# Query and weight steps that wait once a tile's estimate of VectorE time is used up

## The chip, the cores and the metric

The program runs on one core of a Trainium2 chip. Its time is the device time of one execution in microseconds (us). The kernel before takes 1639.06 us, the median of three runs from 1638.23 to 1640.07.

Names of the engines: PE is TensorE, DVE is VectorE, ACT is ScalarE, POOL is GpSimd, SP is the engine that issues the DMAs. Each works through its own queue in the order in which the program wrote it, and waits for the others by semaphores.

## What is computed

Attention through 32 packed queries per head, then two feed-forward layers over 4608 tokens of width 512. Everything is float32.

```python
def sm_attn(qq, kk, vv):
    s = scale * np.matmul(qq, kk.transpose(0, 1, 3, 2))
    a = np.exp(s - np.max(s, axis=-1, keepdims=True))
    a = a / (np.sum(a, axis=-1, keepdims=True) + 1e-09)
    return np.matmul(a, vv)
p_packed = sm_attn(p, k, v)
x = sm_attn(q, p_packed, p_packed)       # 8 batches x 8 heads x 576 x 64
# x is laid out as 4608 rows of 512
xn = x / np.sqrt(np.mean(x * x, axis=-1, keepdims=True) + 1e-06) * rms_g
g, val = xn @ w_gate, xn @ w_val          # 512 -> 1536
y = (g / (1 + np.exp(-g)) * val) @ w_out  # 1536 -> 512
h = y @ w_in                              # 512 -> 2048
out = (np.maximum(h, 0) + alpha * np.minimum(h, 0)) @ w_out2
```

## The kernel before

Every product is made of three matmuls: an operand is split into a high part (ACT, line 109) and the rest (DVE, line 112, or POOL, line 361), and `mm3` multiplies high by high, high by low and low by high (lines 121 to 123).

The first feed-forward layer goes over the tokens in twelve chunks, c = 0 to 11, of 512 or 320 tokens. Chunks 0, 4, 7 and 10 have 512, the others 320. A chunk is a loop over f = 0 to 11, one tile of 128 of the 1536 hidden columns each. A tile has this backbone, in the order in which it is written:

- PE makes `ps_g` (six matmuls for 320 tokens of one batch), ACT takes its tanh (line 1057), DVE does the gate step on it (line 1062), PE makes `ps_v` (six more), DVE multiplies (line 1066), ACT and DVE split the product into `hh` and `hl`;
- PE multiplies the *previous* tile's `hh` and `hl` into the four sums `ps_y` (`blk_out(f - 1)`), 12 matmuls;
- `both` prepares the next block of output weights, `in_h` on ACT, `in_l` on POOL or, from chunk 7 on, by a load.

The rest of the work of chunks 1 to 11 is optional in each tile: it has to be done some time in the chunk, and is fitted in between.

- A *query chain* (`q_steps`) prepares 256 tokens (or 64) of the next chunk: two transposes of scores (line 623), the maximum (625), the subtraction (627), the exponential on ACT (631), the sum and its reciprocal (633 to 635), the product (637), the transpose back `A2T` (642), then matmuls with it on PE (653) and squares on ACT (677). Steps are marked by kind: E is elementwise on DVE, X is the exponential, R reads a result of PE out of PSUM, M is a maximum of the other kind of chain. The *key chain* (`k_steps`) does the same for the keys of a later batch.
- `work(f, at)` moves these chains on at four places of a tile. at = 1 lies between the tanh and the gate step, at = 2 after `hl`, at = 3 after the first `burst`, at = 4 after the second. `burst(f, 2)` and `burst(f, 3)` issue the chains' matmuls on PE, the first just before `blk_out`, the second behind it.
- `late_step` moves the conversion of the second layer's weights on by one step (`conv_late`, 113 steps in all): of every seven, three narrow 64-bit words to floats (lines 224, 228, 230, 233) and four form sums of weight blocks on POOL (line 281) and split them into `w7o` (ACT 109, DVE 112), which SP stores to DRAM (line 278). There are two buffers `w7o`: the third split waits until the first one's store has landed. A table `EVERY` says after how many tiles a step is due at the end of a tile (every tile in chunks 1, 8, 9), `TWICE` adds steps in the middle of a tile in chunks 4, 7 and 10.

The four PSUM banks that `ps_g`, `ps_v`, `ps_at` and `ps_wg` share go round in turn, so PE can't begin a block before the one four places back has been read.

The second layer (from about 916 us on) isn't touched by any of this.

Of the kernel before, what the change touches and what calls it, by code (L numbers as in the profile page):

```python
# [18 lines left out]
def attention_moe_moe2_kernel(ctx, tc, q, k, v, p, w_gate, w_val, w_out, rms_g, w_in2, w_out2, alpha, out):  # L19
    nc = tc.nc  # L20
    B, H, S, D = q.shape
# [4 lines left out]
    T = 512  # L26
# [34 lines left out]
    tiles, of_chunk = [], []  # L61
    for t0, n, cuts in CH:
        groups = []
        for lo, hi, b in cuts:
            for o in range(lo, hi, 256):
                ids = []
# [7 lines left out]
    for i in range(NP1):  # L74
        b, r = i // 3 * 2, i % 3
# [49 lines left out]
    with tc.manual_schedule():  # L125
# [44 lines left out]
        def load_q(i):  # L170
            if i >= len(tiles):
                return
            if hold[0] is not None:
                hold[0].append(i)
                return
            t = ap.tile([128, H * D], F32, tag="q", name="qt", bufs=NQ)
            b, s = divmod(tiles[i][0], S)
            n = tiles[i][1]
            nc.sync.dma_start(
                out=t[0:n].rearrange("p (h d) -> p h d", h=H),  # L180
                in_=q[b, :, s:s + n, :].rearrange("h p d -> p h d"),
            )
            q_t[i] = t
# [157 lines left out]
        def conv(n):  # L341
            for _ in range(n):
                next(convs, None)

        def conv_to(n):
            while n_conv[0] < min(n, NU1):
                next(convs)
# [22 lines left out]
        E, X, R, M = -1, -2, -3, -4  # L370

        class Chain:
            def __init__(self, steps, b):
                self.steps, self.b, self.done, self.last = steps, b, 0, None
                self.next()

            def next(self):
                if self.kind_ok() and self.kind > 0:
                    self.done += 1
                self.kind = next(self.steps, None)  # L380
# [11 lines left out]
        chains = {"k": [], "q": []}  # L392
# [9 lines left out]
        def preload(func):  # L402
            nc.scalar.activation(out=tick[0], in_=mhalf, func=func)
# [421 lines left out]
        def hsplit(h, n):  # L825
            hh = ring.tile([128, T], F32R, tag="hh", name="hh")[:, 0:n]
            hl = ring.tile([128, T], F32R, tag="hl", name="hl")[:, 0:n]
            split_hi(hh, h)
            split_lo(hl, h, hh)
            return hh, hl  # L830
# [4 lines left out]
        def load_rows(pr, kk):  # L835
            t0, w = PAIRS[pr]
            rows = []
            for d in (kk, kk + 2):
                t = one.tile([128, 2 * T], F32, tag="w64", name="y_raw", bufs=NST)[:, 0:2 * w]
                nc.sync.dma_start(out=t, in_=y_dram[d, :, t0:t0 + 2 * w])  # L840
                rows += [t[:, 0:w], t[:, w:2 * w]]
            return rows
# [4 lines left out]
        def prep(pr):  # L847
            w = PAIRS[pr][1]

            def operand(n, kk, src):  # L850
                h, l = [p2.tile([128, T], F32R, tag=f"y{x}{n}{kk}", name="y" + x)[:, 0:w] for x in "hl"]
                split_hi(h, src)
                split_lo(l, src, h)
                y_op[OPERANDS.index(n), kk] = (h, l)

            def less(x, y):
                t = (temp() if pr == 0 else one.tile([128, T], F32, tag="w32", name="y_d", bufs=2))[:, 0:w]
                nc.vector.tensor_tensor(out=t, in0=x, in1=y, op=ALU.subtract)
                return t

            for kk in range(2):
                rows = y_rows.pop(0)
                b11, b12, b21, b22 = rows
                t1 = less(b12, b11)
                operand("b11", kk, b11)
                yield
                t2 = less(b22, t1)
                operand("t1", kk, t1)
                yield
                t4 = less(b21, t2)  # L870
                operand("t2", kk, t2)
                yield
                t3 = less(b22, b12)
                operand("t4", kk, t4)
                yield
                operand("t3", kk, t3)
                yield
                operand("b21", kk, b21)
                yield
                operand("b22", kk, b22)  # L880
                if kk == 0:
                    y_rows.append(load_rows(pr, 1))
                    yield
                yield
# [27 lines left out]
        def load_next():  # L912
            if stream:
                kind, i, n = stream.pop()
                t = wa.tile([128, 2, 256], F32R, tag="w", name="w7")
                nc.sync.dma_start(out=t.bitcast(F32), in_=(w7_dram if kind == "i" else o7_dram)[i * 7 + n])
                here.append(((kind, i, n), t))
# [10 lines left out]
        EVERY = {1: 1, 2: 2, 3: 3, 4: 1, 5: 2, 6: 3, 7: 1, 8: 1, 9: 1, 10: 1, 11: 2}  # L928
        TWICE = {4: 4, 7: 2, 10: 2}

        def late_step(c, f, mid):
            every = (TWICE if mid else EVERY).get(c)
            if every and f % every == every - 1:
                next(late, None)

        for c, (t0, n, cuts) in enumerate(CH):
            last = c == NP1 - 1
# [1 line left out]
            if c == 0:  # L939
                chains["k"] = [Chain(k_steps(b, bk_at), b) for b in range(1, B)]  # L940
            nq = [] if last else of_chunk[c + 1]
            chains["q"] = [Chain(q_steps(ids, bk_at), tiles[ids[0]][0] // S) for ids, _ in nq]

            first = [None]

            def work(f, at):
                live = [ch for ch in chains["k"] if ch.kind is not None][:1] + chains["q"]
                swap = c > 0 or at == 3 and any(ch.kind == X or ch.kind == M for ch in live)
                if swap and c == 0:
                    preload(ACTF.Exp)  # L950
                for ch in live:
                    n_ = 0
                    while n_ < 2:
                        if ch.kind == R and (at == 1 or at > 2 and (ch is first[0] or n_ == 0)):
                            pass
                        elif n_ == 0 and ch.kind == E and (c == 0 or at < 4) or swap and ch.kind in (X, M):
                            pass
                        else:
                            break
                        ch.last = (c, f, at)  # L960
                        ch.next()
                        n_ += 1
                if swap and c == 0:
                    preload(ACTF.Silu)
                if c == 0:
                    conv(2 if at < 4 else 0)
# [67 lines left out]
            for f in range(NF):  # L1034
                if c == 0 and f == 1:
                    held, hold[0] = hold[0], None
                    for i in held:
                        load_q(i)
                if c == 3 and f == 0:
                    nc.sync.dma_start(out=alpha_sb, in_=alpha.rearrange("(f p) -> p f", p=128))  # L1040
                if c == 0:
                    j1 = (f + 1) // 2
                    conv_to(min(6 * j1 + (5 if f % 2 else 6), NU1))
                if last:
                    if f == 0:
                        y_rows.append(load_rows(0, 0))
                        prepare = prep(0)
                    if f > 0:
                        next(prepare, None)
                    if f in (2, 3, 8, 9, 10):  # L1050
                        next(prepare, None)
                    if f > 2:
                        load_next()
                tg = blk_in(f, 0, "g")
                s = ring.tile([128, T], F32, tag="s", name="s")[:, 0:n]
                if c:
                    nc.scalar.activation(out=s, in_=tg, func=ACTF.Tanh, scale=0.5)  # L1057
                else:
                    nc.scalar.activation(out=s, in_=tg, func=ACTF.Silu)
                work(f, 1)  # L1060
                if c:
                    nc.vector.scalar_tensor_tensor(  # L1062
                        out=s, in0=s, scalar=1.0, in1=tg, op0=ALU.add, op1=ALU.mult
                    )
                tv = blk_in(f, 256, "v")
                nc.vector.tensor_tensor(out=s, in0=s, in1=tv, op=ALU.mult)  # L1066
                for jb in JOBS[c].get(f, ()) if c else ():
                    wg_job(*jb)
                hs[f] = hsplit(s, n)
                work(f, 2)  # L1070
                burst(f, 2)
                work(f, 3)
                late_step(c, f, True)
                if 0 < f < NF - 1:
                    blk_out(f - 1)
                if f < NF - 1:
                    burst(f, 3)
                    work(f, 4)
                if f < NF - 1:
                    both(("o", f + 1))  # L1080
                late_step(c, f, False)
            tail = [NF - 2, NF - 1]
            if nq:
                for ch in chains["q"]:
# [308 lines left out]
```

## Time and profile before

| | |
|---|---|
| median of 3 runs | 1639.06 us |
| profiled execution, its own time | 1638.71 us |
| its span, first to last instruction | 1636.9 us |
| PE busy | 1569.6 us, 96% |
| DVE busy | 1188.2 us, 73% |
| ACT busy | 891.3 us, 54% |
| POOL busy | 257.6 us, 16% |
| mean granted TensorE clock | 0.989 |

The times of the steps come from the profiled execution. PE is the engine with the least idle time; where it stands still, the views by waits and the timeline say for whom. A matmul's row in the timeline gives its start and its length; the next one's start is often earlier than its end, since matmuls overlap.

### The profile page before, as it was taken

What the parts mean: (1) busy time and instruction counts of PE and PEld (TensorE: products, weight loads), DVE (VectorE), ACT (ScalarE), POOL (GpSimd) and SP (SyncE); (2) the same over time, 40 slices, a digit from 0 to 9 for tenths busy, and PEclk for the clock granted to TensorE, in tenths of its full rate; (3) what the DMA queues carried; (4) which work ended last, traced back from release to release, by engine and by line L of the source; (5) the groups of instructions that cost most, each with busy time, mean ns of one, the idle gap of its engine ahead of it and who ended that gap; (6) DMA issues with size and microseconds to landing.
All of it is one profiled execution on the core that took longest, in us unless ns stands there. A gap on an engine that the chain in (4) does not pass through costs nothing.

```text
span 1636.9 us, 31939 instructions
## 1 busy us (share of the span) xinstructions
PE 1569.6 (96%) x11786; PEld 1377.2 (84%) x11786; DVE 1188.2 (73%) x2244; ACT 891.3 (54%) x1906; POOL 257.6 (16%) x238
## 2 busy tenths in 40 slices
PE   6689999999999999998999999999999999999999
PEld 4466887888778887888888888988998899999999
DVE  5787667666776766766766778867886787788785
ACT  4566555555465454665555546545654555565564
POOL 1442333232333312212121000000000000000000
PEclk9899999999999999999999999999999999999999
DMA  9876766626565365885645667766777667788876
GB/s 250 270 230 195 219 180 183 165 65 185 178 181 184 112 212 188 263 265 165 218 160 201 213 192 212 230 214 192 212 228 216 208 188 238 259 267 278 265 244 199
DMA packets 230426, 340.55 MB, mean 208 GB/s; under 512 B 62464, under 2 KB 96256, under 8 KB 230272
## 3 DMA queue, kind: packets, MB, share of 16 engines
q1 hardware_dynamic: 230272, 338.51, 67.0%
q8 instruction: 94, 1.54, 0.4%
q14 instruction: 60, 0.49, 0.1%
HBM read 280.77 MB, written 57.67 MB: 207 GB/s over the span
## 4 chain that ended last, share of the span: by engine, by line
PE 60%; DVE 12%; ACT 6%; issue 2%; DMA 2%; DVEq 0%; ACTq 0%; SPq 0%
PE ps_g L121 11%; PE ps_g L122 11%; PE ps_g L123 11%; PE ps_y L121 7%; PE ps_y L123 6%; PE ps_y L122 6%; DVE hl L112 2%; PE ps_wg L730 2%; PE ps_v L121 1%; PE ps_v L122 1%; PE ps_v L123 1%; DVE s L1066 1%; ACT hh L109 1%; DVE s L1062 1%; DMA w_dram<-w7o 1%
## 5 line engine op out<-in xcount | busy, mean ns | idle before, releaser
L121 PE MATMUL ps_y<-hh,in_h 128*128 128x320 f32 (+1 forms) x576 | 208.7, 362 | 4.0 <-ACT hh L109 4.0
L121 PE MATMUL ps_g<-yh,w 128*128 128x512 f32 (+1 forms) x560 | 206.5, 369 | 0.5 <-DVE tmp L1137 0.5
L122 PE MATMUL ps_g<-yl,w 128*128 128x512 f32 (+1 forms) x560 | 206.3, 368 | 0.0
L123 PE MATMUL ps_g<-yh,w 128*128 128x512 f32 (+1 forms) x560 | 205.7, 367 | 0.0
L122 PE MATMUL ps_y<-hl,in_h 128*128 128x320 f32 (+1 forms) x576 | 198.1, 344 | 3.2 <-DVE hl L112 2.6
L123 PE MATMUL ps_y<-hh,in_l 128*128 128x320 f32 (+1 forms) x576 | 196.5, 341 | 0.0
L109 ACT ACTIVATE hh<-s 128x320 fp32r<-128x320 f32 (+1 forms) x144 | 75.6, 525 | 189.5 <-DVE s L1066 189.4
L109 ACT ACTIVATE hh<-kept 128x512 fp32r<-128x512 f32 (+1 forms) x200 | 116.4, 587 | 102.1 <-PE ps_g L122 49.2
L123 PE MATMUL ps_y<-w,hl 128*128 128x256 f32 x576 | 164.7, 286 | 3.1 <-DVE hl L112 2.3
L122 PE MATMUL ps_y<-w,hh 128*128 128x256 f32 x576 | 162.7, 282 | 0.0
L121 PE MATMUL ps_y<-w,hh 128*128 128x256 f32 x576 | 162.4, 282 | 0.0
L121 PEld LDWEIGHTS ps_y<-hh,in_h 128*128 128x128 f32 x576 | 110.4, 192 | 57.8 <-issue 41.6
L361 POOL TENSOR_TENSOR in_l<-w_raw,in_h 128x512 fp32r<-128x512 f32 x72 | 95.8, 1330 | 278.7 <-ACT in_h L109 243.0
L112 DVE TENSOR_TENSOR hl<-kept,hh 128x512 fp32r<-128x512 f32 (+1 forms) x200 | 123.2, 631 | 16.0 <-ACT hh L109 14.9
L1137 DVE TENSOR_TENSOR tmp<-tmp,ps_g 128x512 f32<-128x512 f32 (+2 forms) x140 | 88.3, 631 | 55.2 <-PE ps_g L123 55.2
L112 DVE TENSOR_TENSOR hl<-s,hh 128x320 fp32r<-128x320 f32 (+1 forms) x144 | 82.5, 573 | 60.7 <-ACT hh L109 60.7
L121 PE MATMUL ps_g<-xh,wgh 128*128 128x256 f32 (+3 forms) x352 | 113.1, 321 | 10.4 <-ACT pT L116 3.2
L123 PE MATMUL ps_g<-w,hl 128*128 128x256 f32 x432 | 122.4, 283 | 0.0
L122 PE MATMUL ps_g<-w,hh 128*128 128x256 f32 x432 | 122.2, 283 | 0.0
L121 PE MATMUL ps_g<-w,hh 128*128 128x256 f32 x432 | 122.2, 283 | 0.0
L122 PEld LDWEIGHTS ps_y<-hl,in_h 128*128 128x128 f32 x576 | 110.6, 192 | 13.6 <-DVE hl L112 7.0
L1062 DVE SCALAR_TENSOR_TENSOR s<-s,ps_g 128x320 f32<-128x320 f32 (+1 forms) x132 | 70.9, 537 | 67.1 <-ACT s L1057 66.4
(197 smaller groups left out, 4204.0 us busy)
## 6 DMA issues: line engine op xcount, KB each, us to landing
w<-w_dram SPq DMA_DIRECT2D x280, 256.0 KB, 3.1
w<-o_dram SPq DMA_DIRECT2D x280, 256.0 KB, 3.0
gv_raw<-gv_dram SPq DMA_DIRECT2D x168, 256.0 KB, 3.9
in_l<-lo_dram SPq DMA_DIRECT2D x59, 256.0 KB, 3.9
w<-in_moe_w_out_dram SPq DMA_DIRECT2D x28, 512.0 KB, 5.0
w_dram<-w7o SPq DMA_DIRECT2D x56, 256.0 KB, 2.9
o_dram<-w7o SPq DMA_DIRECT2D x56, 256.0 KB, 2.6
vt<-in_v_dram SPq DMA_DIRECT2D x16, 576.0 KB, 5.9
```

The costliest lines, as they stand in the source:

```text
L109: nc.scalar.activation(out=hi, in_=src, func=ACTF.Copy)
L112: nc.vector.tensor_tensor(out=lo, in0=src, in1=hi.bitcast(F32), op=ALU.subtract)
L121: nc.tensor.matmul(out=o, lhsT=lh, rhs=rh, start=first, stop=False, skip_group_check=more)
L122: nc.tensor.matmul(out=o, lhsT=lh, rhs=rl, start=False, stop=False, skip_group_check=more)
L123: nc.tensor.matmul(out=o, lhsT=ll, rhs=rh, start=False, stop=last, skip_group_check=more)
L361: nc.gpsimd.tensor_tensor(out=l, in0=raw[u], in1=h.bitcast(F32), op=ALU.subtract)
L730: nc.tensor.matmul(out=ts[g][h * NP:(h + 1) * NP, :], lhsT=ppG[b][e * D:(e + 1) * D, c_, :], rhs=us[c_][e * D:(e + 1) * D, :], start=True, ...
L1062: nc.vector.scalar_tensor_tensor(out=s, in0=s, scalar=1.0, in1=tg, op0=ALU.add, op1=ALU.mult)
L1066: nc.vector.tensor_tensor(out=s, in0=s, in1=tv, op=ALU.mult)
L1137: nc.vector.tensor_tensor(out=out, in0=x, in1=y, op=ALU.add)
```

## The change

Three things are added. First, `spent` counts an estimate of the optional DVE time of a tile: 0.7 for each E or R step of a chain of 256 tokens (in proportion for a smaller one, 0.35 for a key chain), 0.9 for an M step, 1.0 for a late step. It is set to zero right behind the steps at at = 1. Second, an E step is only done while `spent` is under a limit: 2.2 in a chunk of 320 tokens, 3.4 in one of 512, without limit in chunks 0 and 11. R and M steps are counted and never held, X steps are neither counted nor held. Third, a late step that is due while the limit is reached is owed, and made up at the next place, which may now be the middle of a tile in any chunk.

```diff
         class Chain:
-            def __init__(self, steps, b):
-                self.steps, self.b, self.done, self.last = steps, b, 0, None
+            def __init__(self, steps, b, w=0.5):
+                self.steps, self.b, self.done, self.last, self.w = steps, b, 0, None, w
                 self.next()
...
-        def late_step(c, f, mid):
+        spent, owed = [0.0], [0]
+
+        def late_step(c, f, mid, limit):
             every = (TWICE if mid else EVERY).get(c)
-            if every and f % every == every - 1:
+            owed[0] += bool(every and f % every == every - 1)
+            if owed[0] and spent[0] < limit:
+                owed[0] -= 1
+                spent[0] += 1.0
                 next(late, None)
...
-            chains["q"] = [Chain(q_steps(ids, bk_at), tiles[ids[0]][0] // S) for ids, _ in nq]
+            chains["q"] = [
+                Chain(q_steps(ids, bk_at), tiles[ids[0]][0] // S, sum(tiles[i][1] for i in ids) / 256) for ids, _ in nq
+            ]
 
             first = [None]
+            limit = 1e9 if c == 0 or last else 2.2 if n < T else 3.4
...
-                        elif n_ == 0 and ch.kind == E and (c == 0 or at < 4) or swap and ch.kind in (X, M):
+                        elif n_ == 0 and ch.kind == E and (c == 0 or at < 4) and spent[0] < limit:
+                            pass
+                        elif swap and ch.kind in (X, M):
                             pass
                         else:
                             break
                         ch.last = (c, f, at)
+                        if ch.kind != X:
+                            spent[0] += 0.9 if ch.kind == M else 0.7 * ch.w
                         ch.next()
...
                 work(f, 1)
+                spent[0] = 0.0
...
-                late_step(c, f, True)
+                late_step(c, f, True, limit)
...
-                late_step(c, f, False)
+                late_step(c, f, False, limit)
```

What this moves is seen in the written order of two queues in chunk 9, whose 320 tokens stand beside two query chains of 256.

DVE in chunk 9, from the `hl` of tile 2 to the `hl` of tile 3, in the kernel before. `A_9376` is the first query chain, `A_9448` the second, `w_9410` and `w_9474` are late steps, lines 1062 and 1066 are the gate step and the product.

```order
L112 TENSOR_TENSOR hl<-s,hh 128x320
L627 TENSOR_TENSOR A_9376<-A_9376,s_9287 128x512
L633 TENSOR_REDUCE s_9287<-A_9376 128x16
L634 TENSOR_SCALAR s_9287<-s_9287 128x16
L635 RECIPROCAL s_9287<-s_9287 128x16
L623 STREAM_TRANSPOSE A_9448<-ps_at 128x256 x2
L230 SCALAR_TENSOR_TENSOR w_9410<-w_9021,w_9410 128x512
L224 TENSOR_SCALAR w_9474<-w_9069 128x512
L637 TENSOR_TENSOR A_9376<-A_9376,s_9287 128x512
L625 TENSOR_REDUCE s_9288<-A_9448 128x16
L1062 SCALAR_TENSOR_TENSOR s<-s,ps_g 128x320
```

The same stretch of DVE now (the second chain is called `A_9443`; the gate step is line 1075):

```order
L112 TENSOR_TENSOR hl<-s,hh 128x320
L625 TENSOR_REDUCE s_9287<-A_9376 128x16
L627 TENSOR_TENSOR A_9376<-A_9376,s_9287 128x512
L623 STREAM_TRANSPOSE A_9443<-ps_at 128x256 x2
L1075 SCALAR_TENSOR_TENSOR s<-s,ps_g 128x320
```

Nine rows stood between `hl` and the gate step; three are left. The sum, the reciprocal and the product of the first chain come a tile later, and with them its transpose back, which now follows the `hl` of tile 4 and not of tile 3. The two late steps are owed.

ACT in chunk 9, tiles 6 and 7 of the kernel before: the seven splits of one pair of weight blocks are spread over tiles 4 to 7 (two, one, two, two), and the last four stand here.

```order
L1057 ACTIVATE s<-ps_g 128x320
L109 ACTIVATE hh<-s 128x320
L109 ACTIVATE in_h<-w_raw 128x512
L109 ACTIVATE w7o<-w_9410 128x256 x2
L1057 ACTIVATE s<-ps_g 128x320
L109 ACTIVATE hh<-s 128x320
L109 ACTIVATE in_h<-w_raw 128x512
L109 ACTIVATE w7o<-w_9474 128x256 x2
```

ACT in chunk 9 now, tiles 8 and 9 and the tanh of tile 10 (line 1069 is the tanh):

```order
L1069 ACTIVATE s<-ps_g 128x320
L109 ACTIVATE hh<-s 128x320
L109 ACTIVATE w7o<-w_9538 128x256
L109 ACTIVATE w7o<-w_9598 128x256
L109 ACTIVATE in_h<-w_raw 128x512
L109 ACTIVATE w7o<-w_9598 128x256
L1069 ACTIVATE s<-ps_g 128x320
L109 ACTIVATE hh<-s 128x320
L109 ACTIVATE w7o<-w_9538 128x256 x2
L109 ACTIVATE in_h<-w_raw 128x512
L109 ACTIVATE w7o<-w_9598 128x256 x2
L1069 ACTIVATE s<-ps_g 128x320
```

The seven splits now stand in two tiles, three in tile 8 and four in tile 9, in front of the next tile's tanh.

## Rows read from the trace of the kernel before

**Rows 1.** The page: busy time, share and instructions of each engine.
```profile
PE 1569.6 (96%) x11786; PEld 1377.2 (84%) x11786; DVE 1188.2 (73%) x2244; ACT 891.3 (54%) x1906; POOL 257.6 (16%) x238
```
**Rows 2.** By stretch: PE, PEld, DVE, ACT, POOL busy, clock; chunk 9, second layer.
```profile
729.20:785.60 56.40, 51.33 (x390) 47.22 (x389) 38.22 (x85) 31.64 (x81) 10.32 (x10) 1.00 0.59 186
...
916.20:1636.90 720.70, 713.44 (x4714) 669.88 (x4712) 558.41 (x942) 389.38 (x730) 0.00 (x0) 1.00 0.73 227
```
**Rows 3.** PE's waits in chunks 1 to 10: total, times, longest.
```profile
PE ps_at L653 <- DVE A2T L642: 6.6, 3, 3.3
...
PE ps_g L121 <- DVE s L1062: 1.2, 2, 0.9
...
PE ps_at L653 <- DVE E1T L118: 0.6, 1, 0.6
```
**Rows 4.** Timeline of PE (start, length, [idle <- releaser]): chunks 3, 6, 9.
```profile
327.12 0.48 PE L653 MATMUL ps_at<-ppbd,A2T 64*128 64x128 f32 x2 [0.85 <-DVE A2T L642]
328.16 1.25 PE L653 MATMUL ps_at<-ppbd,A2T 64*128 64x128 f32 x14 [0.55 <-DVE E1T L118]
...
543.38 1.44 PE L653 MATMUL ps_at<-ppbd,A2T 64*128 64x128 f32 x16 [2.43 <-DVE A2T L642]
...
742.64 0.31 PE L121 MATMUL ps_v<-xh,wgh 128*128 128x320 f32 x1
...
746.90 0.31 PE L123 MATMUL ps_v<-xh,wgl 128*128 128x320 f32 x1
750.48 1.16 PE L653 MATMUL ps_at<-ppbd,A2T 64*128 64x128 f32 x16 [3.27 <-DVE A2T L642]
```
**Rows 5.** Timeline of ACT and DVE: chunk 9's tile 3.
```profile
743.70 0.42 ACT L1057 ACTIVATE s<-ps_g 128x320 f32<-128x320 f32 x1
...
744.49 0.65 DVE L230 SCALAR_TENSOR_TENSOR w<-w,w 128x512 int32<-128x512 int32 x1
...
745.39 1.80 DVE L637 TENSOR_TENSOR A<-A,s 128x512 f32<-128x512 f32 x1
747.12 0.67 DVE L625 TENSOR_REDUCE s<-A 128x16 f32<-128x512 f32 x1
747.71 0.47 DVE L1062 SCALAR_TENSOR_TENSOR s<-s,ps_g 128x320 f32<-128x320 f32 x1
...
749.72 0.70 DVE L642 STREAM_TRANSPOSE A2T<-A 128x512 f32<-128x512 f32 x1
```
**Rows 6.** By stretch, behind the waits of chunks 3, 6 and 9.
```profile
329.10:332.50 3.40, 3.40 (x14) 3.18 (x13) 2.94 (x5) 0.31 (x2) 1.07 (x1) 0.50 0.01 2
...
544.10:547.50 3.40, 3.40 (x19) 3.18 (x17) 2.80 (x5) 1.31 (x3) 1.28 (x1) 0.50 0.06 22
...
748.90:752.30 3.40, 1.82 (x21) 1.70 (x22) 2.29 (x4) 1.65 (x4) 0.00 (x0) 1.00 0.00 0
```
**Rows 7.** Timeline of ACT: two tanhs, and splits that wait.
```profile
773.69 0.42 ACT L1057 ACTIVATE s<-ps_g 128x320 f32<-128x320 f32 x1
...
776.71 0.42 ACT L1057 ACTIVATE s<-ps_g 128x320 f32<-128x320 f32 x1
...
765.94 0.71 ACT L109 ACTIVATE w7o<-w 128x256 fp32r<-128x256 f32 x2
...
770.32 0.42 ACT L109 ACTIVATE w7o<-w 128x256 fp32r<-128x256 f32 x1 [0.35 <-DMA o_dram<-w7o]
...
823.86 0.42 ACT L109 ACTIVATE w7o<-w 128x256 fp32r<-128x256 f32 x1
...
829.05 0.42 ACT L109 ACTIVATE w7o<-w 128x256 fp32r<-128x256 f32 x1 [3.89 <-DMA o_dram<-w7o]
```
**Rows 8.** The stores of `w7o`: from issue to landing.
```profile
DMA to landing us min/median/max: 2.0/2.7/5.8
```
**Rows 9.** Timeline of POOL in chunk 9: two adds.
```profile
745.27 1.37 POOL L233 TENSOR_TENSOR w<-w,w 128x512 int32<-128x512 int32 x1 [17.26 <-issue]
...
760.82 0.98 POOL L281 TENSOR_TENSOR w<-w,w 128x256 f32<-128x256 f32 x1
```

## The prediction

> **What bounds the kernel now.** I read the page first: PE is busy 96% of the span, DVE 73% [rows 1]. So time is won only where PE stands still. The view by stretches says where the change can act: the second layer is 720.7 us in which nothing moves, and PE is busy 713.4 of them; chunk 9 lasts 56.4 us with PE busy for 51.3, DVE for 38.2 [rows 2]. DVE has room as a mean there, so what PE loses it loses to a queue that is full for a moment. The view of PE's waits over chunks 1 to 10 names it: the largest is `A2T`, the transpose back of a query chain, three times, 6.6 us; next to it come waits for the gate step (1.2) and for a copy of a key chain (0.6) [rows 3]. The timeline puts the three waits for `A2T` into chunks 3, 6 and 9 (0.85, 2.43 and 3.27 us), each before the first matmul of line 653, and the wait for the copy behind the first of them (0.55) [rows 4]. These are the chunks of 320 tokens beside two query chains of 256.
>
> Then the timeline of DVE before the last of them shows why `A2T` was late. The tanh of tile 3 ended at 744.12, the gate step began at 747.71: 3.6 us in which DVE did a late step (744.49 to 745.39, 0.90), and then the two steps at at = 1: the product of the first chain (1.80) and the maximum of the second (0.59 until the gate step) [rows 5]. `A2T` begins 2.01 us behind the gate step's start and takes 0.70 [rows 5].
>
> **The terms.** Without these 0.90 and 2.32 (745.39 to 747.71) the gate step of tile 3 would begin at 744.49, 0.4 us behind its tanh. By the written order the change does take both away from there.
>
> How much of the wait goes? PE comes to line 653 after 30 matmuls: rest of the tile's `ps_v`, `blk_out` and the next pair, 742.64 to 746.90 plus one more of (746.90 - 742.64) / 29 = 0.147, so 4.4 us behind the end of `ps_g` [rows 4]. On DVE the way from there is tanh 0.42, then 2.01 and 0.70 [rows 5]: 3.1, with small gaps 3.2. So 1.2 us are to spare if the gate step is on time. It won't be quite: `A2T` of chunk 9 now follows tile 4, and between the gate steps of tiles 3 and 4 stand the sum, the maximum, the product and the subtraction. At start-to-start times of 1.1 for the sum with its reciprocal and 0.6 for each other (the maximum's 0.59, rows 5), 2.9, plus the 2.01, that is 4.9 us against a tile of 24 matmuls, 3.5 us: 1.4 late, 0.2 more than there is to spare. I leave 0.8 of the wait standing for gaps, and count the 0.9 that PE then waited for the gate step [rows 3] as gone: 3.27 + 0.9 - 0.8 = 3.4 us in chunk 9. In chunk 6 the transpose back stands behind two steps of 0.6 that it didn't have before it, which just uses the 1.2 up: of 2.43 I count 2.0. In chunk 3 one such step is new, and a late step and a maximum leave: of 0.85 + 0.55 I count 1.2. Sum 6.6; bounds from nothing (the wait only moves with the step) to all, 8.0.
>
> The clock. Right behind the waits of chunks 3 and 6 the granted clock was 0.50, that is 1.2 of 2.4 GHz, for 3.4 us each, with PE busy throughout; behind the longer wait of chunk 9 it stayed at 1.00 [rows 6]. At half clock such a stretch loses 1.7 us of matmuls. If the waits shrink, both can go: 3.4; since the longest wait had no fall, the tie isn't firm, and I count three quarters, 2.5. Bounds 0 and 3.4.
>
> What it adds. Late steps that are owed are made up close together. In chunk 9 the four steps that split weight blocks stood in four tiles; now seven splits stand in tiles 8 and 9, three and four, each in front of a tanh. There are two buffers, so a split waits for the store of the one two before. In the trace this took 4.1 us from start to start in chunk 9 (the second of the pair at 766.23, to 770.32) and 5.2 in chunk 10 (823.86 to 829.05), where ACT stood for 3.89 us [rows 7]; the least that the parts allow is 0.42 for the split, as much on DVE, and a landing of 2.0 [rows 8], 2.8. In chunk 10 the tile was long and hid it; here it isn't. Undisturbed, a tile of ACT and DVE takes 3.02 us from tanh to tanh with one late step in it [rows 7], PE's takes 3.5. With a pair of splits as long as a late step (0.71, rows 7), tile 8 comes to 3.4, tile 9 to 3.7, and tile 10, which gets two narrowing steps, to 3.7: 10.8 against PE's 10.6. On top come the waits: the third split would follow the first by 1.3 (its pair and one more operation of 0.6), the fifth the third by 2.6, the sixth the fourth by 1.3, the seventh the sixth at once. At 2.8 they wait 1.5 + 0.2 + 1.5 = 3.2, at 5.2 3.9 + 2.6 + 3.9 = 10.4, at 4.1 7.1. PE notices when `hl` is late by more than its reserve, which is 4.4 + 0.15 - 2.6 = 1.9 at best (the same count as above, to the end of `hl`). So PE loses 10.8 - 10.6 - 1.9 = -1.7 plus the waits: 1.5 to 8.7, 5.4 by the value of chunk 9. That value is of the second split of a pair, whose store is issued behind the first's; the first comes back sooner, so I take 4.0.
>
> The same crowding in chunk 1 (five splits in tiles 7 and 8) has tiles of 6 us and I price it at 0, at most 2. In chunks 4, 7 and 10 DVE's steps move within tiles of 7 to 9 us where no wait for `A2T` was: nothing, cover the length of the tile. In chunks 2, 5 and 8 steps move from in front of the gate step to behind `hl`; no wait of theirs is large in rows 3: nothing, bounds 1 either way. SP's stores move with their splits, and a load of `in_l` for the next block can come behind a pair of them in the middle of a tile; it is used more than half a tile later, so nothing unless the store itself waits, which is in the term above.
>
> The sum, made on the profiled execution's own 1638.71, which is 0.35 below the median: -6.6 - 2.5 + 4.0 = -5.1, so 1633.6; with the offset 1634.
>
> A rule of the Trainium skill speaks against the change here. The row: DVE's product took 1.80 us, from 745.39, beside an add on POOL from 745.27 to 746.64 [rows 5, 9], where the maximum behind it took 0.67. "SBUF — State Buffer", section "SBUF: two separate sides", says that a DVE operation with two SBUF inputs and a GpSimd operation that reads SBUF exclude each other for the whole instruction. The row agrees. By that rule the four sums of blocks that POOL does within those two tiles of chunk 9 (up to 0.98 each, rows 9) could hold up DVE by as much each time, 3.9 us in all; the sum would then be about -1.
>
> **The rivals.**
>
> *The gain is eaten.* The crowded splits cost what the waits for `A2T` give back, or PE's wait moves with `A2T`: the transpose back still comes right behind some `hl` and just before its matmuls. For it: DVE has the same number of instructions; 4.9 us against 3.5 in the one tile that matters. Against it: three of the four long stretches before a gate step get shorter by 2 us or more. Time: -9.1 + 7 to 9, or -3 + 2: 1637 to 1639, say 1638.
>
> *Slower: ACT stands behind the stores.* One mechanism, in chunk 9's tiles 8 to 10: a split that waits for a landing holds the tanh behind it, so the gate step, `hl`, and PE. At 5.2 us per buffer PE loses 8.7, and 2 in chunk 1. For it: ACT stood 3.89 us in just this pattern [rows 7]. Against it: in chunk 9 itself the wait was 0.35. It decides once it costs more than the gain: with waits for `A2T` that shrink to half (-4.0) and no clock regained, 10.7 - 4.0 = +6.7 at worst, 1645; likely 1643.
>
> *The change doesn't do what it says.* The estimate counts steps that cost DVE nothing (an R step that only ACT reads counts 0.7), so it holds steps too early, and the limits may merely shift work. Then the same as before, 1639, and the written order speaks against it, since nine rows before a gate step became three.
>
> **How the numbers follow.** What a measurement of this kernel can tell from no change is about 0.2%, 3.3 us. My forecast, 1634, has a chance of 0.54 and spreads from 1628 (all waits and both clock stretches back, 11.4, crowding at its least, 1.5) to 1636. The gain eaten: 0.22, 1638. Not doing what it says: 0.04. Slower by the stores: 0.20, 1643. Hence faster 0.53, within 0.2% 0.27, slower 0.20. The range for 8 in 10 goes from 1628 to 1643.
>
> **What would show it.** Right: in PE's waits of chunks 1 to 10 the row for `A2T` falls from 6.6 to under 2, no stretch at clock 0.50 in chunks 3 and 6, chunk 6 shorter by 3 to 4 us, chunk 3 by 2 to 3. The term of the stores: new idle time of ACT before `w7o` in chunk 9's tiles 8 and 9, 3 to 7 us, and PE waiting for `hh`, `hl` or a bank in its tiles 9 to 11. Wrong: the wait for `A2T` as long as before in tile 5 in place of 4; ACT's waits there without any of PE, which makes it faster than I say; or chunk 9 longer than 56.4 us, which makes the slower rival right.

## The result, and the profile after

The changed kernel takes 1653.28 us (median of four runs, 1652.57 to 1658.87) against 1639.23 (1638.23 to 1640.07) of the kernel before, a ratio of 1.0091 with an interval of 1.0073 to 1.0109. It is 14 us slower. 1634 was predicted, with a range from 1628 to 1643: the sign was wrong, and the time lies outside the range.

The profiled execution of the change took 1653.99 us, 15.3 more than that of the kernel before, as the spans say too (1652.2 less 1636.9). Busy time of each engine first, to be laid beside [rows 1]:

```profile
PE 1580.7 (96%) x11786; PEld 1382.5 (84%) x11786; DVE 1188.6 (72%) x2244; ACT 892.0 (54%) x1906; POOL 257.2 (16%) x238
```

The instructions are the same in number, and DVE and ACT have the same work to within 0.7 us. So nothing was added; time was lost in waiting, or at the lower clock.

A chunk runs from its first matmul to that of the next. In us, from one profiled execution of each kernel; the last two columns are two experiments of the next section:

| chunk | before | change | e3 | e11 |
|---|---|---|---|---|
| 1 | 73.98 | 73.02 | 73.12 | 72.33 |
| 2 | 66.88 | 64.35 | 65.62 | 68.56 |
| 3 | 65.98 | 62.94 | 61.22 | 61.78 |
| 4 | 88.65 | 89.54 | 88.98 | 88.80 |
| 5 | 62.93 | 65.61 | 66.60 | 66.13 |
| 6 | 62.99 | 64.75 | 61.55 | 60.76 |
| 7 | 86.08 | 88.53 | 85.38 | 85.38 |
| 8 | 57.14 | 59.98 | 58.52 | 58.04 |
| 9 | 56.42 | 60.59 | 57.22 | 52.34 |
| 10 | 79.36 | 84.38 | 80.23 | 79.54 |
| sum | 700.4 | 713.7 | 698.4 | 693.7 |

Chunks 1 to 10 lost 13.3 us. The other 2.0 lie ahead of chunk 1, in work that the change leaves in its order; they differ between executions of the experiments as well (chunk 0 began anywhere from 48.7 to 50.9 us), so I don't count them as an effect of the change. In chunks 1 to 7 the key chains' matmuls moved between chunks, so their single differences are mixed. Chunks 8 to 10 have no key chain: 12.0 us of pure loss.

The stretches of the change, in the order of columns of [rows 2]: chunks 1 to 10, chunk 9, second layer.

```profile
166.60:880.30 713.70, 684.16 (x5810) 575.58 (x5808) 478.06 (x1010) 379.15 (x913) 195.96 (x182) 0.99 0.57 180
...
735.30:795.90 60.60, 54.45 (x390) 49.60 (x389) 38.12 (x84) 33.03 (x82) 10.10 (x10) 0.95 0.55 178
...
931.40:1652.20 720.80, 713.51 (x4714) 669.86 (x4712) 558.51 (x943) 389.48 (x730) 0.00 (x0) 1.00 0.72 227
```

The second layer is unchanged to 0.1 us. Chunk 9, from which the prediction drew most of its gain, is 4.2 longer, with the same DVE time (38.1 for 38.2) and a clock of 0.95 for 1.00.

PE's waits in chunks 1 to 10 of the change, as [rows 3]:

```profile
PE ps_at L653 <- DVE A2T L642: 5.7, 3, 2.9
...
PE ps_y L122 <- DVE hl L112: 3.2, 7, 0.9
PE ps_y L121 <- ACT hh L109: 3.1, 3, 1.3
PE ps_at L663 <- DVE A2T L642: 2.1, 1, 2.1
PE ps_wg L730 <- DVE s L1075: 1.6, 1, 1.6
```

The wait for `A2T` was to fall from 6.6 to under 2. It is 5.7, and a fourth wait for a transpose back (line 663) makes it 7.8. The timeline of PE shows where the two long ones lie, in chunks 6 and 9, one tile later than in [rows 4]; that of chunk 3 is gone:

```profile
548.97 1.16 PE L653 MATMUL ps_at<-ppbd,A2T 64*128 64x128 f32 x16 [2.86 <-DVE A2T L642]
...
752.13 0.31 PE L123 MATMUL ps_g<-xh,wgl 128*128 128x320 f32 x1
...
759.36 1.91 PE L653 MATMUL ps_at<-ppbd,A2T 64*128 64x128 f32 x16 [2.51 <-DVE A2T L642]
```

Why `A2T` is late again is read from ACT and not from DVE. ACT in chunk 9, tiles 3 and 4 (line 631 is the exponential of a query chain, 1069 the tanh):

```profile
748.58 0.63 ACT L631 ACTIVATE A<-A 128x512 f32<-128x512 f32 x1 [1.88 <-DVE A L627]
749.12 0.62 ACT L109 ACTIVATE in_h<-w_raw 128x512 fp32r<-128x512 f32 x1
749.64 0.42 ACT L1069 ACTIVATE s<-ps_g 128x320 f32<-128x320 f32 x1
...
755.06 0.63 ACT L631 ACTIVATE A<-A 128x512 f32<-128x512 f32 x1 [3.39 <-DVE A L627]
755.60 0.62 ACT L109 ACTIVATE in_h<-w_raw 128x512 fp32r<-128x512 f32 x1
756.12 0.42 ACT L1069 ACTIVATE s<-ps_g 128x320 f32<-128x320 f32 x1
```

and DVE in the same tiles (line 1075 is the gate step):

```profile
750.09 0.49 DVE L1075 SCALAR_TENSOR_TENSOR s<-s,ps_g 128x320 f32<-128x320 f32 x1 [0.85 <-ACT s L1069]
...
751.71 0.49 DVE L112 TENSOR_TENSOR hl<-s,hh 128x320 fp32r<-128x320 f32 x1 [0.54 <-ACT hh L109]
752.12 0.68 DVE L633 TENSOR_REDUCE s<-A 128x16 f32<-128x512 f32 x1
...
753.75 0.68 DVE L637 TENSOR_TENSOR A<-A,s 128x512 f32<-128x512 f32 x1
754.35 0.69 DVE L627 TENSOR_TENSOR A<-A,s 128x512 f32<-128x512 f32 x1
756.57 0.49 DVE L1075 SCALAR_TENSOR_TENSOR s<-s,ps_g 128x320 f32<-128x320 f32 x1 [1.54 <-ACT s L1069]
...
758.60 0.70 DVE L642 STREAM_TRANSPOSE A2T<-A 128x512 f32<-128x512 f32 x1
```

The last matmul of tile 4's `ps_g` began at 752.13 and took 0.31; its tanh began at 756.12, 3.7 us behind it. ACT had stood still for 3.39 us, until 755.06, for the subtraction (line 627) of the second chain, since that chain's exponential is ahead of the tanh in its queue. The subtraction is the last of six steps that DVE had been given behind `hl`. Then exponential, `in_h` and tanh follow each other on ACT, and DVE has nothing to do for 1.54 us. So the chain is: held steps pile up behind `hl`; the exponential, which is neither counted nor held, waits on ACT for the end of the pile; the tanh waits behind it; the gate step and `A2T` come late.

The end of chunk 9 is another place. ACT, the splits of tiles 8 and 9 that wait for a store, and the tanh of tile 10:

```profile
779.12 0.42 ACT L109 ACTIVATE w7o<-w 128x256 fp32r<-128x256 f32 x1 [2.22 <-DMA o_dram<-w7o]
...
781.91 0.42 ACT L109 ACTIVATE w7o<-w 128x256 fp32r<-128x256 f32 x1 [0.43 <-DMA o_dram<-w7o]
783.09 0.42 ACT L109 ACTIVATE w7o<-w 128x256 fp32r<-128x256 f32 x1 [0.76 <-DMA o_dram<-w7o]
...
784.92 0.42 ACT L109 ACTIVATE w7o<-w 128x256 fp32r<-128x256 f32 x1 [0.89 <-DMA o_dram<-w7o]
786.09 0.42 ACT L109 ACTIVATE w7o<-w 128x256 fp32r<-128x256 f32 x1 [0.76 <-DMA o_dram<-w7o]
786.42 0.42 ACT L1069 ACTIVATE s<-ps_g 128x320 f32<-128x320 f32 x1
```

and PE behind them:

```profile
787.42 1.65 PE L730 MATMUL ps_wg<-gv_raw,ppG 64*32 64x512 f32 x16 [1.58 <-DVE s L1075]
...
792.11 0.42 PE L121 MATMUL ps_y<-hh,in_h 128*128 128x320 f32 x1 [1.08 <-ACT hh L109]
793.20 0.41 PE L122 MATMUL ps_y<-hl,in_h 128*128 128x320 f32 x1 [0.68 <-DVE hl L112]
```

ACT waits 5.06 us in all, and PE then waits for a bank that the late gate step frees (1.58), for `hh` and for `hl`. The mechanism that the prediction priced at +4.0 is there, where it was expected.

In chunk 10 the transpose back of a 64-token chain, now written ahead of the gate step, stands on DVE behind a split that waits for a store on ACT (3.18); this is PE's wait of 2.1 at line 663:

```profile
839.88 0.42 ACT L109 ACTIVATE w7o<-w 128x256 fp32r<-128x256 f32 x1 [3.18 <-DMA o_dram<-w7o]
...
840.67 0.30 DVE L642 STREAM_TRANSPOSE A2T<-A 128x128 f32<-128x128 f32 x1
```

In the kernel before, ACT's wait for that store was longer (3.89 [rows 7]), but the transpose back stood right behind `hl`, ahead of the splits, and PE had no wait here.

And the clock, as [rows 6], behind these three places:

```profile
759.50:762.90 3.40, 3.40 (x22) 3.18 (x23) 2.71 (x7) 0.50 (x3) 0.00 (x0) 0.51 0.02 5
793.60:797.00 3.40, 3.40 (x17) 3.40 (x16) 3.12 (x5) 2.26 (x6) 1.59 (x1) 0.52 1.02 367
841.40:844.80 3.40, 3.40 (x9) 2.11 (x8) 2.12 (x4) 1.23 (x3) 0.00 (x0) 0.51 0.51 163
```

The two stretches at half clock in chunks 3 and 6 are gone, and three have come in chunks 9 and 10 (the second reaches from one into the other): one more stretch at 1.2 GHz than before.

### The profile page after: what moved, and what is told of

Read it like the earlier page. It is cut to its first block, busy times and chain, and to the rows that moved or that the text cites. A ratio compares the mean times of both kernels' runs of the same rounds, so it can differ in the third digit from the quotient of the medians.

```text
span 1652.2 us, 31931 instructions
## 1 busy us (share of the span) xinstructions
PE 1580.7 (96%) x11786; PEld 1382.5 (84%) x11786; DVE 1188.6 (72%) x2244; ACT 892.0 (54%) x1906; POOL 257.2 (16%) x238
## 3 DMA queue, kind: packets, MB, share of 16 engines
q8 instruction: 94, 1.54, 0.4%
## 4 chain that ended last, share of the span: by engine, by line
PE 66%; DVE 17%; ACT 7%; DMA 5%; issue 3%; SPq 2%; POOL 0%; DVEq 0%; ACTq 0%; POOLq 0%
PE ps_g L121 11%; PE ps_g L122 11%; PE ps_g L123 11%; PE ps_y L121 7%; PE ps_y L123 7%; PE ps_y L122 7%; PE ps_wg L730 3%; DVE hl L112 3%; DVE s L1079 2%; PE ps_v L121 2%; ACT hh L109 2%; PE ps_v L122 2%; PE ps_v L123 2%; DMA w_dram<-w7o 2%; DVE s L1075 1%
```

## The experiments

The theory: the exponential in front of the tanh on ACT costs most of it. The rivals: the owed late steps, crowded together, cost it; or holding the E steps is bad by itself. Every kernel is an edit of the changed one unless said; times are medians, ratios are to the kernel before on the same chip.

**e1: late steps done when due, as before the change.** E steps are still held.

```diff
-            if owed[0] and spent[0] < limit:
+            if owed[0]:
```

> The change, but late steps are done when the tables say so, as in the kernel before; only the elementwise query steps are held. Theory of the stores (seven splits of weight blocks crowded into tiles 8 and 9 of chunk 9 make ScalarE wait for the stores and TensorE with it): tiles 10 and 11 of chunk 9 fall back from 4.25 and 11.99 us to about 3.5 and 7.1, the whole to 1646 to 1648. Theory of the exponential (it stands in ScalarE's queue before the next tanh and waits there for VectorE's last step of the tile): this run stays at 1651 to 1654, since the exponentials are where the change put them.

1649.21 us, ratio 1.0052 (1.0037 to 1.0067), between the ranges of the two theories: neither is the whole. It gives back 0.39 of the 0.91 per cent. Chunk 9 comes to 57.09, but the wait for `A2T` is still there, and chunk 10 keeps 84.28. The crowding is a part; 0.52 per cent of loss remain without it.

**e2: only the late steps wait; E steps aren't held.**

```diff
-... ch.kind == E and (c == 0 or at < 4) and spent[0] < limit:
+... ch.kind == E and (c == 0 or at < 4):
```

> The other half alone: late steps are held and made up, elementwise query steps are done as in the kernel before (the estimate still counts them). Theory of the stores: in chunk 9 five splits stand in tiles 7 and 8, so 2 to 4 us of wait there, 1641 to 1644 in all. Theory of the exponential: no exponential moves, so 1638 to 1640.

1646.90, ratio 1.0041 (1.0026 to 1.0056). Late steps alone lose 3.3 us in chunk 3, 1.6 in chunk 6 and 2.9 in chunk 9, and nothing in chunk 10: that chunk's 5 us need the held E steps. The time lies above what either theory expected, also when it is counted from the 1640.99 us of the kernel before on this chip. ACT's waits before exponentials are as in the kernel before (22.8 and 11.4 us at lines 631 and 457), so no exponential did this; what the owed late steps cost outside chunk 9 was in neither theory.

**e3: the exponential only at the places at = 1 and 2.** At at = 1 it stands behind the tanh on ACT, and at at = 2 it comes early; all else is as in the change.

```diff
-                        elif swap and ch.kind in (X, M):
+                        elif swap and (ch.kind == M or ch.kind == X and (c == 0 or at < 3)):
```

> The change, but in chunks 1 to 11 an exponential is only issued at the first two places of a tile (behind the tanh or behind hl), so at the next tile's first place instead of in front of its tanh; nothing else of the chains moves. Theory of the exponential: TensorE's wait for A2T in chunks 6 and 9 (3.0 and 2.7 us) goes under 1 each, ScalarE's waits for L627 and L448 fall from 51 us to under 25, the whole to 1644 to 1648. Theory of the stores: 1651 to 1654, the waits of chunk 9's tiles 10 and 11 stay.

1638.23, ratio 0.9982 (0.9972 to 0.9992). One line takes back all of the loss, 1.09 per cent of the time, and more than the theory expected (1644 to 1648). ACT's waits for the last step before an exponential, chunks 1 to 10; first the kernel before, then the change, then e3 (line 631 query, 457 key):

```profile
ACT A L631 <- DVE A L627: 22.2, 19, 1.8
...
ACT E L457 <- DVE st L448: 11.4, 7, 2.4
```
```profile
ACT A L631 <- DVE A L627: 28.7, 15, 3.4
...
ACT E L457 <- DVE st L448: 22.4, 11, 3.4
```
```profile
ACT A L631 <- DVE A L627: 6.9, 5, 1.8
...
ACT E L457 <- DVE st L448: 1.0, 2, 0.8
```

33.6 us before, 51.1 with the change, 7.9 in e3. All of these waits before and with the change lie in front of a tanh. What the change did is to make them longer: for query chains they are rarer, but up to 3.4 us in place of 1.8. How it looks in e3 at the place of the rows above (ACT, DVE and PE, tiles 3 and 4 of chunk 9):

```profile
743.63 0.44 ACT L1069 ACTIVATE s<-ps_g 128x320 f32<-128x320 f32 x1 [0.39 <-PE ps_g L123]
745.56 0.63 ACT L631 ACTIVATE A<-A 128x512 f32<-128x512 f32 x1 [1.49 <-DVE A L627]
...
744.84 0.69 DVE L627 TENSOR_TENSOR A<-A,s 128x512 f32<-128x512 f32 x1
745.45 0.48 DVE L1075 SCALAR_TENSOR_TENSOR s<-s,ps_g 128x320 f32<-128x320 f32 x1
...
748.22 1.16 PE L653 MATMUL ps_at<-ppbd,A2T 64*128 64x128 f32 x16 [0.28 <-DVE A2T L642]
```

DVE's pile behind `hl` is the same six steps, but the tanh now comes first, the gate step follows the pile without a gap, and PE waits 0.28 us for `A2T` in place of 2.51. Over chunks 1 to 10 PE's wait for `A2T` at line 653 falls from 5.7 to 0.5.

Not all that e3 takes back is ACT's queue in front of a tanh. Its edit also shifts when the later steps of a chain fall due. In chunk 10 the small chain's transpose back stands behind `hl` again (829.85), ahead of the splits' remainders (830.07), and PE's wait at line 663 is gone; chunk 10 is 4.2 us shorter than with the change.

**e8 and e10: the same for the query chains alone, and for the key chains alone.**

```diff
+e8:  ... ch.kind == X and (c == 0 or at < 3 or ch in chains["k"])):
+e10: ... ch.kind == X and (c == 0 or at < 3 or ch in chains["q"])):
```

> The change, with the query chains' exponentials alone kept to the first two places; the key chains' stay where the change put them. ScalarE's waits in front of exponentials are 28.7 us for query chains and 22.4 for key chains with the change, 22.2 and 11.4 before. The theory of the exponential says that the 15 us that e3_exp_early got back divide between the two: by these waits some 9 here, 1643 to 1646.

> The counterpart: the change, with the key chains' exponentials alone kept to the first two places. By the same waits some 6 us back, 1645 to 1649; chunks 8 to 10 have no key chain, so their loss (12 us by the profile) stays as it is, and the gain lies in chunks 2 to 7. If it is under 2 us the key chains have no part in it.

e8: 1644.68, ratio 1.0017 (1.0007 to 1.0027). e10: 1647.29, ratio 1.0030 (1.0016 to 1.0044). Of 0.91 per cent the first takes back 0.74, the second 0.61. Both kinds matter, and each has a share of half or more; together they overlap a little (1.35 for 1.09).

**e5: the kernel before, with the same rule for the exponential.**

> The kernel before, with the one edit that an exponential is only issued at the first two places of a tile in chunks 1 to 11; no step is held. It moves the key chains' exponentials off the fourth place, the query chains' stay at the second. If holding steps has a gain of its own, this is 1638 to 1641, slower than e6_both by 2 us or more. If all of e6_both's gain is the exponential's, this is 1635 to 1637.

1642.46, ratio 1.0006 (0.9996 to 1.0016): no gain, and a little above both expected ranges, as is the kernel before on this chip (1641.18). ACT's wait at line 631 is the same row as before, 22.2 us in 19 times: in the kernel before no query exponential stood at the late places, the rule moves key exponentials alone there, and those did no harm. The query exponentials came to the late places by the change, which holds the subtraction back. So the rule is no improvement by itself: what e3 takes back is what the change did.

**e6: e1 and e3 together.**

> Both edits: late steps as in the kernel before, exponentials only at the first two places, elementwise steps held by the estimate. If stores and exponentials explain the loss, 1636 to 1640, and below 1639 if holding the steps has a gain of its own. Rival, that the later place of the elementwise steps itself costs (less room before their matmuls): 1645 or more.

1636.43, ratio 0.9972 (0.9962 to 0.9982). Holding the E steps is a gain once neither side effect is there: 0.34 per cent below e5. That holding is bad by itself is refuted. The owed late steps cost 0.41 per cent by themselves (e2) and 0.39 on top of held steps (the change against e1), but only 0.10, with intervals that overlap, once the exponentials are early (e3 against e6). So the two side effects are not independent.

**e11: e3, and owed late steps made up only at a tile's end** in chunks that have no steps of their own in the middle.

```diff
-            if owed[0] and spent[0] < limit:
+            if owed[0] and spent[0] < limit and (not mid or every or c == NP1 - 1):
```

> e3_exp_early (exponentials early, late steps held and owed), but what is owed is made up at a tile's end only, except in chunks 4, 7, 10 and 11, so that no short tile gets two late steps. Theory of the stores: the two to three us that chunk 9 still loses in e3_exp_early against e6_both come back there, so chunk 9 at 55 to 56 us in place of 57.2, and 1636 to 1638 in all. If the stores have no part, 1638 to 1640 as e3_exp_early.

1634.49, ratio 0.9952 (0.9936 to 0.9967): faster than both kernels, and than expected. Chunk 9 in e3 and then in e11, columns as in [rows 2]:

```profile
726.40:783.60 57.20, 52.54 (x390) 47.32 (x389) 36.99 (x84) 32.72 (x81) 9.38 (x10) 1.00 0.56 183
```
```profile
728.90:781.30 52.40, 51.20 (x391) 47.17 (x390) 35.11 (x79) 30.54 (x77) 7.15 (x8) 1.00 0.54 170
```

4.9 us go from chunk 9 when the splits are at most one pair a tile (ACT's waits for stores there fall from 5.2 to 1.0 us). But this is not the crowding alone: two splits and four of DVE's eight narrowing operations go to chunk 10 (which is none the longer for it). In e6, which leaves as much work in chunk 9 as e3, it takes 54.92, 2.3 less than in e3; there PE still waits 1.79 us for `A2T`, 1.5 more than in e3. So the crowding's price in chunk 9 lies between 3.8 (2.3 + 1.5) and 4.9, an estimate from these rows. Over the whole program e11 is 0.30 per cent, some 5 us, below e3.

**e9: e6 with one limit, 3.4, for all chunks.**

> e6_both with the limit 3.4 in place of 2.2 in the chunks of 320 tokens too, so that steps are held less there. If holding gains by itself, 1636.5 to 1639, between e6_both and the kernel before; if the limit is a mere shift, the same as e6_both, 1635.5 to 1637.

1639.71, ratio 0.9991 (0.9979 to 1.0003). Most of the gain of e6 is lost, but its runs spread from 1636.4 to 1644.0 us, so the size is uncertain.

**e12 and e14: e6 without any E step at at = 1; then that without the limit too.**

```diff
-... ch.kind == E and (c == 0 or at < 4) and spent[0] < limit:
+e12: ... ch.kind == E and (c == 0 or 1 < at < 4) and spent[0] < limit:
+e14: ... ch.kind == E and (c == 0 or 1 < at < 4):
```

> e6_both, and no elementwise step of a query chain stands in front of a gate step any more (the first place of a tile is left out). It moves few steps, mostly in the chunks of 512 tokens. If the place in front of the gate step costs by itself, 1634 to 1636; if not, as e6_both, 1636 to 1637.

> e12_behind_hl without the estimate: no limit, elementwise steps at the second and third place of every tile, exponentials at the first two, late steps as in the kernel before. If the gain of e6_both comes from the place (nothing in front of the gate step), it stays: 1635 to 1637. If it comes from the estimate, that is from holding steps when a tile is full, it goes: 1639 to 1642.

1636.35, ratio 0.9977 (0.9967 to 0.9987), and 1636.83, ratio 0.9982 (0.9973 to 0.9991). Had the estimate itself mattered, e14 would have lost most of e12's gain; it hardly differs from e12 and e6. From e5 it differs only in that no E step stands between the tanh and the gate step, and it is 0.24 per cent faster, with intervals that don't overlap. So what helps is the place; the estimate of the time spent adds nothing that these runs can tell.

More buffers `w7o` would test the stores by themselves; no run has them.

## Why the prediction was wrong

The failed step is "so 1.2 us are to spare if the gate step is on time", with "I leave 0.8 of the wait standing": the count of the way to `A2T` went along DVE alone. It took for granted that a tanh comes as soon as PE has made `ps_g`, and never asked what the moved subtraction does to the exponential that follows it on ACT.

- *Tile 3's gate step* was to begin 0.4 us behind the end of its tanh. It begins at once: the tanh runs from 749.64 to 750.06, the gate step starts at 750.09. The first half of the step was right.
- *Tile 4*: 2.9 us of DVE steps were counted between `hl` and the gate step. They are there (752.12 to 755.04). But the exponential waits for the last of them, and exponential, `in_h` and tanh then take another 1.5 us in which DVE is idle. This is most of what makes the wait 2.5 in place of 0.8. With the exponential behind the tanh (e3) it is 0.28: the count on DVE held, the queue that it left out didn't.
- *The term of the waits and the clock* (-6.6 and -2.5, in chunks 3, 6 and 9). In the change these chunks make -3.0, +1.8 and +4.2. In e11, with both side effects away, -4.2, -2.2 and -4.1, that is -10.5 for the -9.1 forecast, and no stretch at half clock in chunks 1 to 10 but one at 242.6 in chunk 2. That the two numbers are near is in part luck: chunk 9 of e11 has less work, and key-chain work moved between chunks 1 and 7 (chunks 2 and 5 are 1.7 and 3.2 longer). In e6, with late steps as in the kernel before, chunks 3, 6 and 9 take 64.69, 61.74 and 54.92, together only 4.0 less. What the runs do show is the wait itself: 6.6 us for `A2T` at line 653 before, 0.5 in e3 and in e11. The forecast of "under 2" holds once the exponential is behind the tanh; the change as written doesn't reach it. The price of the clock, 1.7 a stretch, was an upper bound, as the last section shows.
- *The crowded splits* (+4.0, bounds 1.5 to 8.7) cost 3.8 to 4.9 in chunk 9. The waits sum to 5.06 us, midway between the 3.2 of the lower bound and the 7.1 of chunk 9's value; by the prediction's own sum (10.8 - 10.6 - 1.9, plus the waits) that makes 3.4. So this term was right in mechanism and near in size.
- *"Nothing" for chunks 4, 7 and 10 and for 2, 5 and 8, "bounds 1 either way"*. Chunk 8 lost 2.8, chunk 10 5.0 us, two thirds of the loss in chunks 8 to 10; e3 leaves 1.4 and 0.9 of them. These terms were put at nothing, and failed for the same reason: their cover, the length of the tile, was counted for DVE's steps, not for ACT's queue.
- *The slower rival* had the sign and one true mechanism, and chunk 9 became longer than 56.4, which by the text made it right. It isn't the whole: by e1 it makes 0.39 of the 0.91 per cent, and with the crowding in place and the exponential moved (e3) the kernel is 0.18 per cent faster than before. Its price of 1643 left the exponential out.
- *"The change doesn't do what it says"* had a true remark in it: X steps aren't counted. It was read as harmless.
- The rule of the Trainium skill ("SBUF — State Buffer", section "SBUF: two separate sides"), which would have added 3.9: DVE's product took 0.68 us at 753.75 with POOL idle, against 1.80 beside POOL's add [rows 5, 9], so the trace still agrees. In chunk 9's tiles 8 and 9 nothing of the 3.9 is seen, but the rule was hardly tested there: while POOL made its four sums (777.08 to 780.89), DVE's only steps with two inputs from SBUF were the end of a split's remainder that had begun before them, and one remainder at 779.57, just as the third sum ended (0.43, as elsewhere).
- A slip in the sums: the fastest case, 11.4 gained and 1.5 lost, gives 1629 and not 1628.

What stays open: chunk 5 is 2.7 to 3.7 us longer in the change, e3 and e11; in e2, e5 and e9, where E steps are held less or not at all, it is as long as before (62.7 to 63.0). The key chains' matmuls moved between chunks 1 and 7, which a table by chunk can't tell from a loss. Of the loss in chunks 1 to 10, PE's busy time is 4.7 us (684.2 less 679.5); one more stretch at half clock explains up to 1.7 of it, the rest isn't settled. Nor can the shares of exponential and crowding be added exactly, as e1, e2, e8 and e10 show.

## What to carry to other kernels

When a step is moved on one engine, follow its *consumer* on the next engine: in a queue that runs in order, a consumer that comes early and waits holds everything behind it, here the tanh that the critical path needs. A budget of one engine's time is not enough to place work by; what must also be asked is who stands in front of whom on every other queue. And work that is put off needs a rule for how it is made up: several steps that share two buffers, done in a row, turn hidden store time into a wait.

## What the runs showed of the hardware

- The length of a wait did not tell whether the clock falls. Behind PE's wait of 2.51 us in chunk 9 it went to 0.51, behind one of 2.86 in chunk 6 it stayed at 1.00 (chunk 6 of the change has no such stretch); in the kernel before it was 0.50 behind 2.43 and 1.00 behind 3.27 [rows 4, 6]. This could not be forecast from the rows.
- A stretch at half clock did not always cost time. e6, e12 and e14 have the same written order on DVE in chunk 9, and PE waits 1.79 us for `A2T` in each; behind it the clock stayed at 1.00 in e6 and fell to 0.50 in e12 and e14. In the stretch behind the wait PE worked on 29 matmuls in e6 and on 18 in e12, and yet chunk 9 took 54.92, 54.92 and 54.93 us: PE's next waits were shorter or gone (a wait of 0.32 us at line 653 gone, one of 1.09 us at line 689 now 0.50). So 3.4 us at half clock cost 1.7 us at most, and here nothing that shows in the chunk's time. e6 and then e12, columns as in [rows 2]:

```profile
752.30:755.70 3.40, 3.40 (x29) 3.27 (x26) 2.72 (x7) 0.77 (x3) 1.60 (x2) 1.00 0.41 146
```
```profile
751.50:754.90 3.40, 3.40 (x18) 3.18 (x16) 2.73 (x7) 0.80 (x3) 1.58 (x2) 0.50 0.42 147
```

- A `w7o` buffer came round in 3.0 us from split to split (781.91 to 784.92, 783.09 to 786.09) when the stores were issued 1.2 us apart, where 4.1 and 5.2 had been read from pairs [rows 7]. Two stores issued 0.4 us apart, at 777.03 and 777.40, landed after 2.01 and 4.41 us.
